# The gates of chunks 2 to 5 split between two engines in the first batch of an mLSTM and mixer kernel

## The chip, the cores and the metric

The kernel runs on one core of one Trainium2 chip. A core has five engines that work side by side, each through its own instructions in order: TensorE (PE, matmuls; PEld are its weight loads), VectorE (DVE), ScalarE (ACT), GpSimd (POOL) and SyncE (SP, which here only issues loads and stores). They meet through semaphores. SBUF is the memory on the core, PSUM the small memory that TensorE writes to. The metric is the device time of one execution in microseconds.

## The reference

Four batches, eight heads, 768 steps, head size 40. First an mLSTM layer with stabilised exponential gates, then a two-part mixer on its output.

```python
for t in range(S):                                   # the mLSTM
    m_new = max(f_gate[t] + m, i_gate[t])
    f_stab = exp(f_gate[t] + m - m_new)
    i_stab = exp(i_gate[t] - m_new)
    m = m_new
    C = f_stab * C + i_stab * outer(v[t], k[t])      # a 40x40 state for each head
    n = f_stab * n + i_stab * k[t]
    y[t] = sigmoid(o_gate[t]) * (C @ q[t]) / max(abs(n . q[t]), 1)
x  = y as (batch, 768, 320)                          # the mixer
u  = x + (relu(x.T @ w_tok1) @ w_tok2).T
out = u + relu(u @ w_ch1) @ w_ch2
```

## The kernel before

The 768 steps of a batch are cut into six chunks of 128. For a chunk the recurrence becomes matrix products: the scores of the chunk's queries and keys, weighted by a decay matrix; a product with the values; and the state carried from chunk to chunk. A pair of a batch and a chunk is a unit; u0, u1 and u2 are the first three. The mixer's matmuls fill most of the run; the first batch's six chunks come ahead of them, up to about 50 us.

The gates are computed once, for all four batches and eight heads together, with a row for each pair (36 partitions; a batch has nine, one of them spare) and the steps along the row. `gates_of` (L115) does it for a range of chunks, all on VectorE: a scan for the running maximum m (L119), the forget gate relative to it (an addition, L124, and a subtraction, L126), a scan that sums it up from each chunk's start to phi (L128, where `rst2` is zero at a chunk's first step), and two subtractions for b (L130, L132). phi and b are the two halves of the tile z. `split` (L170) then takes from the nine rows of the first batch what a bfloat16 does not hold, twice (L172, L173), so that TensorE can spread them exactly.

TensorE builds the decay matrices of the first batch from z: `spread_split` (L184) puts phi and b of one chunk into two PSUM tiles by small bfloat16 matmuls (L163, L178, L181). `prep_exp` (L282) takes their exponential on ScalarE, `st_s` (L302) makes the scores, `st_p` (L312) multiplies both on VectorE (L318), `st_pv` (L411) is the product with the values (L426), and `st_state` (L357) the state (L367, L375, L380, L384). `spread_q` (L192) spreads what decays a chunk's queries, `prep_q3` (L265) exponentiates it on ScalarE (L269) and multiplies the queries by it on GpSimd (L274, L275), and `prep_kw` (L291) weights the keys on GpSimd (L298). `x0_ops` (L459) finishes a unit on VectorE (L463 to L472). `sigmoid` (L216) does the output gates on ScalarE and needs another table of functions than the exponentials, so a table load stands ahead of it and another one behind.

No scheduler sets the order: it is written out by hand (`manual_schedule`), and each engine runs its instructions as the code lists them. So lines 831 to 857, the part between the first chunk and the loop over the others, are also the order of every engine there. In it the gates of chunk 1 are computed alone, those of chunks 2 to 5 in one go of 512 steps (L839), and `warm(7)` (L852, L788) puts seven matmuls on zeros in TensorE's way before chunk 2 is spread. At L858 `gp.release()` frees the gate tiles; weights loaded later (L616) take their place.

Of the kernel before, what the change touches and what calls it, by code (L numbers as in the profile page):

```python
# [13 lines left out]
ALU = mybir.AluOpType  # L14
# [3 lines left out]
B, H, S, D = 4, 8, 768, 40  # L18
L = 128
NC = S // L  # L20
# [14 lines left out]
def kernel(ctx: ExitStack, tc: tile.TileContext, gates, qk, q3, kv, og,  # L35
                            wt1, wt2, wc1, wc2, ident, out):
    nc = tc.nc
# [4 lines left out]
    ps_h = ctx.enter_context(tc.tile_pool(name="ps_h", bufs=2, space=PSUM))  # L42
    ps_acc = ctx.enter_context(tc.tile_pool(name="ps_acc", bufs=2, space=PSUM))
    ps_s = ctx.enter_context(tc.tile_pool(name="ps_s", bufs=2, space=PSUM))
    ps_m = ctx.enter_context(tc.tile_pool(name="ps_m", bufs=2, space=PSUM))
# [19 lines left out]
    f_t = gp.tile([B * HP, S], F32, name="f_t")  # L65
    i_t = gp.tile([B * HP, S], F32, name="i_t")
# [7 lines left out]
    z = pp.tile([128, 2, S], F32, name="z")  # L74
    nc.vector.memset(z, 0.0)
    m_t = gp.tile([B * HP, S], F32, name="m_t")
# [3 lines left out]
    rst2 = rst.rearrange("p c t -> p (c t)")  # L80
# [29 lines left out]
    phi, b_t = z[0:B * HP, 0], z[0:B * HP, 1]  # L110
# [4 lines left out]
    def gates_of(c0, c1):  # L115
        lo, hi = c0 * L, c1 * L
        sl, sd, sm = slice(lo, hi), slice(max(lo, 1), hi), slice(max(lo, 1) - 1, hi - 1)
        v = nc.vector
        v.tensor_tensor_scan(m_t[:, sl], f_t[:, sl], i_t[:, sl],  # L119
                             -1e30 if lo == 0 else m_t[:, lo - 1:lo], op0=ALU.add, op1=ALU.max)  # L120
        yield
        if lo == 0:
            v.memset(f_t[:, 0:1], 0.0)
        v.tensor_tensor(f_t[:, sd], f_t[:, sd], m_t[:, sm], ALU.add)  # L124
        yield
        v.tensor_tensor(f_t[:, sd], f_t[:, sd], m_t[:, sd], ALU.subtract)  # L126
        yield
        v.tensor_tensor_scan(phi[:, sl], rst2[:, 0:hi - lo], f_t[:, sl], 0.0, op0=ALU.mult, op1=ALU.add)  # L128
        yield
        v.tensor_tensor(b_t[:, sl], i_t[:, sl], m_t[:, sl], ALU.subtract)  # L130
        yield
        v.tensor_tensor(b_t[:, sl], b_t[:, sl], phi[:, sl], ALU.subtract)  # L132
        yield

    def cols_w0(t, c):
        a, e = c * L, (c + 1) * L
        nc.tensor.matmul(t, top(z[:, 1, a:e]), id3, start=True, stop=False)
        nc.tensor.matmul(t, top(z[:, 0, e - 1:e]).to_broadcast([128, 128]), id3, start=False, stop=True)

    def cols_w0_out(t, c):  # L140
        nc.scalar.activation(wcol[:, c, 0:HP].rearrange("p (g i) -> p i g", g=3),
                             t.rearrange("p (i g) -> p i g", i=3), AF.Exp)
# [18 lines left out]
    def spread_late(pool, tag):  # L161
        ps = pool.tile([128, 4, L], F32, tag=tag, name="ps_phi")
        nc.tensor.matmul(ps, id_b, late_b.unsqueeze(1).to_broadcast([128, 4, L]), start=True, stop=False)  # L163
        return ps


    def top(x):
        return x.bitcast(BF16).rearrange("... (t i) -> ... t i", i=2)[..., 1]

    def split(c0, c1, eng=nc.vector):  # L170
        p, r, r2 = (z[x:x + HP, :, c0 * L:c1 * L] for x in (0, 64, 96))
        eng.tensor_tensor(r, p, top(p), ALU.subtract)  # L172
        eng.tensor_tensor(r2, r, top(r), ALU.subtract)  # L173
# [10 lines left out]
    def spread_split(u, fill=0):  # L184
        T[u]["phi"] = r = []
        for h in range(0, H, 4):
            r.append(spread_late(ps_h, "h"))
            if fill and h == 0:
                warm(fill)
            spread_phi(r, u[1], h, h + 4)  # L190

    def spread_q(u, pool=(ps_h, "h")):  # L192
        b, c = u
        ps = pool[0].tile([128, 512], F32, tag=pool[1], name="ps_q")
        for g in range(3):
            nc.tensor.matmul(ps[0:120, g * L:(g + 1) * L], sel3[:, g],
                             top(z[:, 0, c * L:(c + 1) * L]), start=True, stop=True)
        T[u]["psq"] = ps[0:120, 0:3 * L].rearrange("p (g t) -> p g t", g=3)
        if c < NC - 1:
            T[u]["psw"] = ps[:, 3 * L:3 * L + HP]  # L200
            cols_w0(T[u]["psw"], c)
# [14 lines left out]
    def sigmoid(b, r=range(2), part=slice(0, 3)):  # L216
        for i in r:
            t = sig[(b, i)][:, part]
            nc.scalar.activation(t, t, AF.Sigmoid)
# [36 lines left out]
    def load_pq(u, q3t):  # L256
        b, c = u
        if c > 0:
            pq = ap.tile([120, 3, L], F32, tag="pq", name="pq", bufs=2)
            if b:  # L260
                nc.sync.dma_start(out=pq.rearrange("p g t -> p (g t)"),
                                  in_=phi_d[c, b * HP:(b + 1) * HP].rearrange("(i g) t -> i (g t)", i=3).unsqueeze(1).to_broadcast([3, D, 3 * L]))
            T[u]["q3"] = (q3t, pq)

    def prep_q3(u):  # L265
        if u[1] == 0:
            return
        q3t, pq = T[u]["q3"]
        nc.scalar.activation(pq, T[u].get("psq", pq), AF.Exp)  # L269
        if "psw" in T[u]:  # L270
            cols_w0_out(T[u]["psw"], u[1])
        if u[1] < NC - 1:
            T[u]["decay"] = a = ap.tile([120, 3], F32, tag="decay", name="decay")
            nc.gpsimd.tensor_copy(a, pq[:, :, L - 1])  # L274
        (nc.vector if u[0] == 1 else nc.gpsimd).tensor_tensor(q3t, q3t, pq, ALU.mult)  # L275
# [6 lines left out]
    def prep_exp(u, hf):  # L282
        b, c = u
        dd = T[u]["dd"]
        if b == 0:
            nc.scalar.activation(dd[:, 4 * hf:4 * hf + 4, :], T[u]["phi"][hf], AF.Exp)
            return
        for h in range(4 * hf, 4 * hf + 4):
            nc.scalar.activation(dd[:, h, :], dd[:, h, :], AF.Exp, bias=bcol[:, c, HP * b + h:HP * b + h + 1])  # L289

    def prep_kw(u):  # L291
        b, c = u
        if c == NC - 1:
            return
        t = T[u]
        kw = ap.tile([128, H * E1], F32, tag="kw", name="kw", bufs=2)
        kw = kw[:, 0:DM].rearrange("p (h d) -> p h d", d=D)
        nc.gpsimd.tensor_tensor(kw, t["kv"][:, 0:DM].rearrange("p (h d) -> p h d", d=D),  # L298
                                wcol[:, c, HP * b:HP * b + H].unsqueeze(2).to_broadcast([128, H, D]), ALU.mult)
        t["kw"] = kw  # L300

    def st_s(u, mult=True, mid=iter(()), rows=64, pool=(ps_s, "s")):  # L302
        t = T[u]
        t["s"] = [pool[0].tile([128, 4, L], F32, tag=pool[1], name="ps_sc") for _ in range(2)]
        for h in range(4):
            for hf in range(2):
                r = t["raw"][64 * hf:64 * hf + rows]
                nc.tensor.matmul(t["s"][hf][:, h, :], r[:, 1, h, :], r[:, 0, h, :], start=True, stop=True)  # L308
        if mult:
            st_p(u, mid)  # L310
# [100 lines left out]
    def st_pv(u, copy=True):  # L411
        b, c = u
        t = T[u]
        vx = t["kv"][:, DM:]
        if "p" in t:
            return st_pv3(u)
        if c:
            po = t["po"]
        else:
            t["bank"] = ps_m.tile([128, 512], F32, tag="m", name="po")  # L420
            po = t["bank"][:, 0:H * E1].rearrange("p (h e) -> p h e", e=E1)
        for h in range(H):
            o, x = po[:, h, :], vx[:, h * E1:(h + 1) * E1]
            if b == 0 and c:
                o, x = po[:, 0:h + 2:h + 1, :], x.unsqueeze(1).to_broadcast([128, 2, E1])
            nc.tensor.matmul(o, t["dd"][:, ROW[h], :], x, start=c == 0 and h == 0, stop=h == H - 1)  # L426
        if b == 0 and c:
            po = po[:, 1:1 + H]
        t["po"] = po
        if b:  # L430
            st_ht(u)
# [75 lines left out]
    u0, u1 = units[0], units[1]  # L507
# [273 lines left out]
    def step(g, n=1):  # L781
        for _ in range(n):
            next(g, None)

    def warm(n, pool=(ps_m, "m"), z=zero):
        t = pool[0].tile([128, 512], F32, tag=pool[1], name="warm")
        for i in range(n):
            nc.tensor.matmul(t[:, 0:z.shape[-1]], z[:, 0:128], z, start=i == 0, stop=i == n - 1)  # L788
# [5 lines left out]
    u0, u1, u2 = us[0:3]  # L794
# [12 lines left out]
    q3s = {u1: load_q3t(u1)}  # L807
# [23 lines left out]
    step(gates_of(1, 2), 9)  # L831
    split(1, 2)
    spread_split(u1, 5)
    st_s(u1, mult=False, pool=(ps_acc, "acc"))
    st_p(u0)
    prep_exp(u1, 0)
    prep_exp(u1, 1)
    sigmoid(0)
    step(gates_of(2, NC), 9)  # L839
    split(2, 3)  # L840
    st_pv(u0)
    x0 = x0_ops(u0)
    step(x0, 2)
    st_state(u0)
    step(x0, 1)
    spread_q(u1, (ps_s, "s"))
    load_pq(u1, q3s[u1])
    prep_q3(u1)
    prep_kw(u1)
    split(3, NC, nc.gpsimd)  # L850
    st_p(u1)
    warm(7, (ps_h, "h"))  # L852
    spread_split(u2)
    prep_exp(u2, 0)
    prep_exp(u2, 1)
# [241 lines left out]
```

## Time and profile before

| | us |
|---|---|
| median of 3 runs | 432.86 |
| lowest and highest | 432.77 and 433.51 |
| the profiled execution, whole | 433.07 |
| its span in the profile | 431.3 |
| PE busy / DVE / ACT / POOL | 425.4 / 291.9 / 185.3 / 141.7 |

The profile gives the start and the duration of every instruction in one execution; times count from the start of the span. The span covers what the engines do, and 1.8 us of the execution lie around it. A row of a timeline may stand for several instructions of one kind: `x6` is their count, and the duration is then from the first's start to the last's end. Names are the program's tiles, `out<-in`, and L is the line of the kernel. Ends of matmuls are modelled, so TensorE looks busy in places where it only waits a little; the starts are measured. The count of matmuls may be one short.

### The profile page before, as it was taken

Reading aid. Unit: us, or ns where it says so; the run is one execution under the profiler, and the core shown is the slowest. Engines: PE = TensorE matmul, PEld = TensorE weight load, DVE = VectorE, ACT = ScalarE, POOL = GpSimd, SP = SyncE. Lnnn points to the kernel's source line nnn. Section 1 sums busy time; section 2 is a strip of 40 time slices with the busy share of each in tenths; the row PEclk is TensorE's granted clock in tenths of the full one; section 3 lists DMA queues with packets and bytes.
Section 4 is the critical chain, followed back from the end, with each engine's and each line's share of the span. In section 5 each row is a group of like instructions: output and inputs, shape, how many; then the busy total and the mean of one; then the engine's idle time right before and its main releaser. Section 6 shows DMA issues by size and latency. Waiting matters only on the chain.

```text
span 431.3 us, 9405 instructions
## 1 busy us (share of the span) xinstructions
PE 425.4 (99%) x3705; PEld 408.0 (95%) x3706; DVE 291.9 (68%) x656; ACT 185.3 (43%) x426; POOL 141.7 (33%) x186
## 2 busy tenths in 40 slices
PE   8999999999999999999999999999999999999996
PEld 4788999999999999999999999999999999999996
DVE  8999877745777788688795688687885645323212
ACT  6877666894544725324414336234334112211111
POOL 7487485860553410341330330332340110000000
PEclk9999999999999999999999999999999999999999
DMA  7988849903877612145356111343240000000000
GB/s 203 278 264 250 270 142 309 291 27 112 225 218 234 204 56 81 67 130 151 96 168 195 59 64 36 125 130 100 94 115 30 2 17 15 2 32 0 27 7 30
DMA packets 24576, 52.37 MB, mean 121 GB/s; under 512 B 2565, under 2 KB 13325, under 8 KB 24533
## 3 DMA queue, kind: packets, MB, share of 16 engines
q1 hardware_dynamic: 24293, 51.61, 38.8%
q8 instruction: 29, 0.48, 0.5%
q10 hardware_dynamic: 240, 0.18, 0.2%
q14 instruction: 14, 0.11, 0.1%
HBM read 47.73 MB, written 4.04 MB: 120 GB/s over the span
## 4 chain that ended last, share of the span: by engine, by line
PE 90%; DMA 4%; DVE 2%; POOL 2%; ACT 1%; issue 1%; ACTq 0%; SPq 0%; POOLq 0%; DVEq 0%
PE ps_h L756 32%; PE acc L675 30%; PE ps_a L675 5%; PE ps_sc L308 5%; PE ps_b L675 5%; PE po L426 4%; PE po L397 3%; PE pu L375 3%; PE po L403 2%; DMA sig<-in_og_dram 2%; DMA id_t<-in_ident_dram 1%; PE po L367 1%; DMA q3t<-in_q_dram 1%; PE ps_t L737 1%; PE ps_t L735 1%
## 5 line engine op out<-in xcount | busy, mean ns | idle before, releaser
L756 PE MATMUL ps_h<-uT,c1h 128*128 128x256 f32 x720 | 137.8, 283 | 0.2
L761 ACT ACTIVATE gh<-ps_h 128x512 fp32r<-128x512 f32 x72 | 43.0, 597 | 177.8 <-PE ps_h L756 177.5
L756 PEld LDWEIGHTS ps_h<-uT,c1h 128*128 128x128 f32 x720 | 114.0, 188 | 1.4 <-DVE uT L739 0.6
L762 DVE SCALAR_TENSOR_TENSOR gl<-ps_h,gh 128x512 fp32r<-128x512 f32 x72 | 49.6, 689 | 91.6 <-ACT gh L761 91.5
L756 PE MATMUL ps_h<-uT,c1l 128*128 128x256 f32 x432 | 108.5, 281 | 0.0
L675 PE MATMUL acc<-c2h,gh 128*128 128x320 f32 x288 | 90.1, 320 | 0.0
L675 PE MATMUL acc<-c2l,gh 128*128 128x320 f32 x288 | 86.7, 309 | 0.0
L756 PEld LDWEIGHTS ps_h<-uT,c1l 128*128 128x128 f32 x432 | 79.7, 188 | 0.3 <-POOL c1l L669 0.3
L675 PE MATMUL acc<-c2h,gl 128*128 128x320 f32 x288 | 65.6, 309 | 0.0
L675 PEld LDWEIGHTS acc<-c2h,gh 128*128 128x128 f32 x288 | 54.1, 188 | 1.6
L675 PEld LDWEIGHTS acc<-c2l,gh 128*128 128x128 f32 x288 | 54.2, 188 | 0.0
L675 PEld LDWEIGHTS acc<-c2h,gl 128*128 128x128 f32 x288 | 48.1, 188 | 0.3 <-DVE gl L762 0.3
L289 ACT ACTIVATE dd<-dd,bcol 128x128 f32<-128x128 f32 x144 | 45.8, 392 | 3.7 <-POOL dd L279 3.5
L445 POOL TENSOR_TENSOR sig<-sig,ht 128x320 f32<-128x320 f32 x18 | 14.6, 814 | 94.7 <-DVE ht L407 87.7
L496 POOL TENSOR_TENSOR xl<-x,xh 128x320 fp32r<-128x320 f32 x18 | 15.8, 878 | 55.4 <-DVE xh L494 54.0
L318 DVE TENSOR_TENSOR dd<-ps_sc,dd 128x512 f32<-128x512 f32 x48 | 30.8, 680 | 1.9 <-PE ps_sc L308 1.9
L308 PE MATMUL ps_sc<-raw 64*128 64x128 f32 (+1 forms) x384 | 28.0, 285 | 0.0
L308 PEld LDWEIGHTS ps_sc<-raw 64*128 64x128 f32 (+1 forms) x384 | 23.4, 187 | 4.1 <-issue 1.9
L279 POOL TENSOR_SCALAR_AFFINE_SELECT dd<-dd 128x1024 f32<-128x1024 f32 x18 | 21.7, 1208 | 10.2 <-DMA dd<-phi_d 10.2
L426 PE MATMUL po<-kvt,dd 128*128 128x41 f32 (+1 forms) x192 | 23.2, 277 | 0.0
L426 PEld LDWEIGHTS po<-kvt,dd 128*128 128x128 f32 x192 | 22.4, 192 | 0.1
L653 DVE SCALAR_TENSOR_TENSOR pf<-pf,wst 128x384 int32<-128x384 int32 x30 | 16.2, 559 | 6.9 <-POOL wst L633 3.4
(147 smaller groups left out, 750.9 us busy)
## 6 DMA issues: line engine op xcount, KB each, us to landing
dd<-phi_d SPq DMA_DIRECT2D x18, 512.0 KB
wst<-in_wc_dram SPq DMA_DIRECT2D x22, 384.0 KB
kvt<-in_kv_dram SPq DMA_DIRECT2D x24, 324.0 KB
raw<-in_qk_dram SPq DMA_DIRECT2D x48, 160.0 KB
sig<-in_og_dram SPq DMA_DIRECT2D x8, 480.0 KB
out_dram<-x SPq DMA_DIRECT2D x24, 160.0 KB
q3t<-in_q_dram SPq DMA_DIRECT2D x20, 180.0 KB
wst<-in_wt_dram SPq DMA_DIRECT2D x8, 384.0 KB
```

Of the source, the lines that this page charges most:

```text
L279: nc.gpsimd.affine_select(dd, dd, pattern=[[0, H], [1, L]], compare_op=ALU.is_ge, fill=-1e30, base=0, channel_multiplier=-1)
L289: nc.scalar.activation(dd[:, h, :], dd[:, h, :], AF.Exp, bias=bcol[:, c, HP * b + h:HP * b + h + 1])
L308: nc.tensor.matmul(t["s"][hf][:, h, :], r[:, 1, h, :], r[:, 0, h, :], start=True, stop=True)
L318: nc.vector.tensor_tensor(dd, t["s"][hf], dd, ALU.mult)
L426: nc.tensor.matmul(o, t["dd"][:, ROW[h], :], x, start=c == 0 and h == 0, stop=h == H - 1)
L445: nc.gpsimd.tensor_tensor(sg, sg, ht[:, :, 0:D], ALU.mult)
L496: nc.gpsimd.tensor_tensor(xl, x, f32(xh), ALU.subtract)
L653: v.scalar_tensor_tensor(fi, fi, 3, raw[:, :, 0], op0=ALU.logical_shift_left, op1=ALU.bitwise_or)
L675: nc.tensor.matmul(ps, a, m, start=(first and i == 0), stop=(last and i == n - 1))
L756: nc.tensor.matmul(ps[:, j, :], c1[x][:, a:a + 128], u[:, y, :], start=part is first and i == 0 and (order == 0 or j == 0), stop=i == len( ...
L761: nc.scalar.activation(gh, ps, AF.Relu)
L762: nc.vector.scalar_tensor_tensor(gl, ps, 0.0, f32(gh), op0=ALU.max, op1=ALU.subtract)
```

## The change

A new generator, `gates_rest`, takes the place of `gates_of` for chunks 2 to 5. The running maximum is still one scan of 512 steps on VectorE. Of what follows VectorE does chunk 2 (128 steps) alone; for chunks 3 to 5 (384 steps) the two additions on f and the two subtractions on b are GpSimd's, and the scan for phi is VectorE's. Chunk 1's query factors (`spread_q`, `load_pq`, `prep_q3`) and key weights (`prep_kw`) move ahead of the sigmoids, the spread of the queries right behind that of phi and into another PSUM pool. The second split of chunks 3 to 5 moves up a little, and the seven matmuls on zeros go.

```diff
--- before.py
+++ after.py
@@ -130,6 +130,24 @@
         v.tensor_tensor(b_t[:, sl], i_t[:, sl], m_t[:, sl], ALU.subtract)
         yield
         v.tensor_tensor(b_t[:, sl], b_t[:, sl], phi[:, sl], ALU.subtract)
+        yield
+
+    def gates_rest():
+        v, p = nc.vector, nc.gpsimd
+        a, z = slice(2 * L, 3 * L), slice(3 * L, S)
+        am, zm = slice(2 * L - 1, 3 * L - 1), slice(3 * L - 1, S - 1)
+        v.tensor_tensor_scan(m_t[:, 2 * L:], f_t[:, 2 * L:], i_t[:, 2 * L:], m_t[:, 2 * L - 1:2 * L],
+                             op0=ALU.add, op1=ALU.max)
+        for e, s, sm in ((v, a, am), (p, z, zm)):
+            e.tensor_tensor(f_t[:, s], f_t[:, s], m_t[:, sm], ALU.add)
+            e.tensor_tensor(f_t[:, s], f_t[:, s], m_t[:, s], ALU.subtract)
+        v.tensor_tensor_scan(phi[:, a], rst2[:, 0:L], f_t[:, a], 0.0, op0=ALU.mult, op1=ALU.add)
+        v.tensor_tensor(b_t[:, a], i_t[:, a], m_t[:, a], ALU.subtract)
+        v.tensor_tensor(b_t[:, a], b_t[:, a], phi[:, a], ALU.subtract)
+        yield
+        p.tensor_tensor(b_t[:, z], i_t[:, z], m_t[:, z], ALU.subtract)
+        v.tensor_tensor_scan(phi[:, z], rst2[:, 0:S - 3 * L], f_t[:, z], 0.0, op0=ALU.mult, op1=ALU.add)
+        p.tensor_tensor(b_t[:, z], b_t[:, z], phi[:, z], ALU.subtract)
         yield
 
     def cols_w0(t, c):
@@ -831,25 +849,26 @@
     step(gates_of(1, 2), 9)
     split(1, 2)
     spread_split(u1, 5)
+    spread_q(u1, (ps_m, "m"))
     st_s(u1, mult=False, pool=(ps_acc, "acc"))
     st_p(u0)
     prep_exp(u1, 0)
     prep_exp(u1, 1)
+    gr = gates_rest()
+    step(gr)
+    load_pq(u1, q3s[u1])
+    prep_q3(u1)
+    prep_kw(u1)
     sigmoid(0)
-    step(gates_of(2, NC), 9)
     split(2, 3)
+    step(gr)
+    split(3, NC, nc.gpsimd)
     st_pv(u0)
     x0 = x0_ops(u0)
     step(x0, 2)
     st_state(u0)
     step(x0, 1)
-    spread_q(u1, (ps_s, "s"))
-    load_pq(u1, q3s[u1])
-    prep_q3(u1)
-    prep_kw(u1)
-    split(3, NC, nc.gpsimd)
     st_p(u1)
-    warm(7, (ps_h, "h"))
     spread_split(u2)
     prep_exp(u2, 0)
     prep_exp(u2, 1)
```

The first place is VectorE, from the maximum's scan (which stands here as a SCALAR_TENSOR_TENSOR) up to x0 of the first unit (L463 before, L481 after). Before:

```order
L119 SCALAR_TENSOR_TENSOR m_t<-f_t,m_t,i_t 36x512
L124 TENSOR_TENSOR f_t<-f_t,m_t 36x512
L126 TENSOR_TENSOR f_t<-f_t,m_t 36x512
L128 SCALAR_TENSOR_TENSOR z<-rst,f_t 36x512
L130 TENSOR_TENSOR z<-i_t,m_t 36x512
L132 TENSOR_TENSOR z<-z 36x512
L172 TENSOR_TENSOR z<-z 9x2x128
L173 TENSOR_TENSOR z<-z 9x2x128
L463 TENSOR_TENSOR po<-po,sig 128x8x40
```

After, with the lines of the changed file:

```order
L139 SCALAR_TENSOR_TENSOR m_t<-f_t,m_t,i_t 36x512
L142 TENSOR_TENSOR f_t<-f_t,m_t 36x128
L143 TENSOR_TENSOR f_t<-f_t,m_t 36x128
L144 SCALAR_TENSOR_TENSOR z<-rst,f_t 36x128
L145 TENSOR_TENSOR z<-i_t,m_t 36x128
L146 TENSOR_TENSOR z<-z 36x128
L190 TENSOR_TENSOR z<-z 9x2x128
L191 TENSOR_TENSOR z<-z 9x2x128
L149 SCALAR_TENSOR_TENSOR z<-rst,f_t 36x384
L481 TENSOR_TENSOR po<-po,sig 128x8x40
```

Five instructions on 512 steps have become five on chunk 2's 128, ahead of the same split of chunk 2; a scan on 384 steps has come in behind the split.

The second place is GpSimd, from the filling of a tile with zeros (the memset) to chunk 0's xl. Before:

```order
L214 MEMSET raw_138 32x1024 x2
L274 COPY decay<-pq 120x3
L275 TENSOR_TENSOR q3t<-q3t,pq 120x384
L298 TENSOR_TENSOR kw<-kvt,wcol 128x320
L172 TENSOR_TENSOR z<-z 9x2x384
L173 TENSOR_TENSOR z<-z 9x2x384
```

After:

```order
L232 MEMSET raw_138 32x1024 x2
L142 TENSOR_TENSOR f_t<-f_t,m_t 36x384
L143 TENSOR_TENSOR f_t<-f_t,m_t 36x384
L292 COPY decay<-pq 120x3
L293 TENSOR_TENSOR q3t<-q3t,pq 120x384
L316 TENSOR_TENSOR kw<-kvt,wcol 128x320
L148 TENSOR_TENSOR z<-i_t,m_t 36x384
L150 TENSOR_TENSOR z<-z 36x384
L190 TENSOR_TENSOR z<-z 9x2x384
L191 TENSOR_TENSOR z<-z 9x2x384
```

Two instructions on f_t stand ahead of chunk 1's query factors and key weights, and two on z between these and the split of chunks 3 to 5; both kinds wait for VectorE at their head.

## Rows read from the trace of the kernel before

**Rows 1.** Timeline of PE: start us, duration us, engine, line, operation, count, [idle before]

```profile
15.33 1.67 PE L788 MATMUL warm<-zero 128*128 128x512 bf16 x6
...
17.18 0.39 PE L178 MATMUL ps_phi<-z,id 128*128 128x128 bf16 x4
```

**Rows 2.** Timeline of DVE, same columns, 10.9 to 17.7 us

```profile
10.97 1.27 DVE L119 TENSOR_TENSOR_SCAN m_t<-f_t,m_t,i_t 36x512 f32<-36x512 f32 x1
...
13.71 1.22 DVE L128 TENSOR_TENSOR_SCAN z<-rst,f_t 36x512 f32<-36x512 f32 x1
...
16.71 0.42 DVE L173 TENSOR_TENSOR z<-z 9x256 f32<-9x256 f32 x1
17.16 0.50 DVE L463 TENSOR_TENSOR po<-po,sig 128x320 f32<-128x320 f32 x1
```

**Rows 3.** Waits of DVE, 17 to 34 us: total us, times, longest us

```profile
DVE pf L653 <- ACT wst L631: 0.6, 1, 0.6
```

**Rows 4.** Timeline of DVE, 25 to 34 us

```profile
32.69 0.49 DVE L472 TENSOR_TENSOR x<-po,den 128x320 f32<-128x320 f32 x1
```

**Rows 5.** Timeline of PE, 31 to 34 us

```profile
33.28 0.80 PE L375 MATMUL pu<-kvt,kw 128*120 128x123 f32 x6 [0.71 <-POOL w1l L669]
```

**Rows 6.** Windows: stretch, length, busy us (instructions) by engine, clock, DMA

```profile
42.00:150.00 108.00, 107.87 (x881) 104.75 (x880) 75.20 (x168) 68.44 (x163) 59.72 (x75) 1.00 0.67 206
428.00:432.00 4.00, 0.02 (x1) 0.00 (x0) 0.49 (x1) 0.00 (x0) 0.00 (x0) 0.81 0.22 82
```

**Rows 7.** Timeline of DVE, 5.4 to 9.8 us

```profile
5.94 0.68 DVE L119 TENSOR_TENSOR_SCAN m_t<-f_t,m_t,i_t 36x128 f32<-36x128 f32 x1
6.65 0.48 DVE L124 TENSOR_TENSOR f_t<-f_t,m_t 36x128 f32<-36x128 f32 x1
7.17 0.28 DVE L126 TENSOR_TENSOR f_t<-f_t,m_t 36x128 f32<-36x128 f32 x1
7.49 0.42 DVE L128 TENSOR_TENSOR_SCAN z<-rst,f_t 36x128 f32<-36x128 f32 x1
...
8.89 0.84 DVE L173 TENSOR_TENSOR z<-z 9x256 f32<-9x256 f32 x1
```

**Rows 8.** Timeline of POOL, 5.5 to 9.6 us

```profile
5.59 0.77 POOL L106 TENSOR_SCALAR_AFFINE_SELECT bm_t<-bm_t 120x369 f32<-120x369 f32 x1
...
6.43 0.58 POOL L106 TENSOR_SCALAR_AFFINE_SELECT bm_t<-bm_t 120x369 f32<-120x369 f32 x1
...
8.73 0.72 POOL L298 TENSOR_TENSOR kw<-kvt,wcol 128x320 f32<-128x320 f32 x1 [1.68 <-ACT wcol L141]
```

**Rows 9.** Timeline of DVE, 149 to 152.7 us

```profile
150.56 0.74 DVE L349 CAST v<-vr 128x328 bf16<-128x328 f32 x1
151.33 1.27 DVE L350 TENSOR_TENSOR v<-vr,v 128x328 bf16<-128x328 f32 x1
```

**Rows 10.** Timeline of POOL, 149 to 152.7 us

```profile
150.12 0.98 POOL L298 TENSOR_TENSOR kw<-kvt,wcol 128x320 f32<-128x320 f32 x1
151.06 1.18 POOL L279 TENSOR_SCALAR_AFFINE_SELECT dd<-dd 128x1024 f32<-128x1024 f32 x1
```

**Rows 11.** Tile vr on DVE: duration ns min/median/max, first and last start us

```profile
L350 DVE TENSOR_TENSOR v<-vr,v x12: 499/501/1267, 151.3 to 334.5; 128x328 bf16<-128x328 f32 x12
```

**Rows 12.** Lines of POOL: instructions xcount | busy us, mean ns | idle before

```profile
L275 POOL TENSOR_TENSOR q3t<-q3t,pq 120x384 f32<-120x384 f32 x15 | 15.2, 1016 | 0.0
...
L147 POOL TENSOR_TENSOR w_row<-z 36x640 f32<-36x640 f32 x1 | 1.3, 1257 | 0.0
```

**Rows 13.** Timeline of ACT, 10.8 to 21 us

```profile
14.66 1.00 ACT L219 ACTIVATE sig<-sig 128x960 f32<-128x960 f32 x1 [0.18 <-DMA sig<-in_og_dram]
...
16.97 0.49 ACT L269 ACTIVATE pq<-ps_q 120x384 f32<-120x384 f32 x1
...
17.82 1.26 ACT L286 ACTIVATE dd<-ps_phi 128x512 f32<-128x512 f32 x2 [0.28 <-PE ps_phi L181]
```

**Rows 14.** Timeline of PE, 1 to 6 us

```profile
1.39 4.45 PE L788 MATMUL warm<-zero 128*128 128x512 bf16 x10 [1.39 <-POOL zero L60]
```

## The prediction

> **What bounds the kernel now.** I read the timelines of the first 35 us first, since the change lies between 5 and 23 us, then the waits of VectorE, then the windows of the rest, to see whether a delay made early comes out at the end.
>
> TensorE stands on zeros from 15.33 until about 17.0 and spreads phi of u2 at 17.18 [rows 1]. VectorE's second split of chunk 2 ends at 16.71 + 0.42 = 17.13 [rows 2], and that is what the zeros cover: a wait for VectorE. Right behind it, at 17.16, VectorE starts L463, the first instruction on u0's output. From there to 33.18, the end of L472 on u2 [rows 4], its only wait of note is 0.6 us, once, on ScalarE [rows 3], and ScalarE gets that work from VectorE's own earlier one. So VectorE bounds 17 to 33 us. The view of TensorE at 33.28 puts a wait of 0.71 us down to GpSimd's w1l [rows 5], but the matmul pu does not read w1l; L472 ended 0.1 us before it and frees the PSUM that pu takes. I read this as TensorE waiting for VectorE. After 42 us TensorE is busy for 107.87 of 108 us [rows 6]: what it is late there it does not make up. A shift of L463 on VectorE therefore moves the end one for one, unless TensorE itself becomes the later one.
>
> **The change part by part.** *VectorE alone.* The scan for m stays and ends at 10.97 + 1.27 = 12.24 [rows 2]; with the gap of 0.03 that lies between two VectorE instructions the next starts at 12.27. Before, 4.9 us of 512-step work and splits followed up to 17.16. After, there are an addition and a subtraction on f, a scan, two subtractions on b, all on 128 steps, and the two splits: by the undisturbed rows of chunk 1 0.28 for an addition or subtraction, 0.42 for a scan [rows 7], and 0.42 for a split [rows 2]. That is 4 × 0.28 + 3 × 0.42 + 7 gaps of 0.03 = 2.6. Then the scan on 384 steps: between 0.42 for 128 [rows 7] and 1.22 for 512 [rows 2] it is 0.95. L463 would start at 15.8, 1.35 us sooner.
>
> *What GpSimd does beside it.* It now has, in this order and from 12.24 on, f+ and f− (384 steps), decay, q3t, kw and b − m, all reading SBUF, while every VectorE instruction of the gates and splits has two inputs in SBUF. Rows 7 and 8 show what such neighbours do. The scan of chunk 1 took 0.68 and ended at 6.62, 0.26 after the affine_select on GpSimd (6.36); the addition took 0.48 and ended 0.12 after the next one (7.01); the split took 0.84 and ended 0.28 after kw (9.45). Alone they take 0.42, 0.28 and 0.42. So VectorE stood still until GpSimd's instruction was over, and only its first 0.14 or so passed beside it. It holds the other way too: at 150 us GpSimd's L279 ended 0.94 after VectorE's L349 did (151.30), and VectorE's L350 ended 0.36 after L279 (152.24), at 1.27 where it mostly takes 0.50 [rows 9 to 11]; kw's L298 there took 0.98 [rows 10] where it took 0.72 [rows 8]. Two queues that both have work take turns, one instruction each.
>
> The Trainium skill, SBUF — State Buffer, "Who interferes with whom", says that a VectorE instruction with two SBUF inputs contends with a GpSimd instruction that reads SBUF, and that whoever comes second waits for the whole of the other. This case's trace agrees on who contends, but shows about 0.14 us of each passing beside the other; without that the sum would be 1.4 us higher.
>
> *The price of a GpSimd instruction on 384 steps* is not in the trace. The nearest rows are q3t, the same 384 elements in a row, in place and from two fp32 inputs, 1.02 on average, and w_row on the same 36 partitions, 640 elements, 1.26 [rows 12]. In proportion the latter gives 0.76 for 384; in full it is a bound from above. I take 1.0, from q3t, which has the same operation and length. Less 0.14 each holds VectorE 0.86 (0.62 and 1.12 at the bounds); kw holds it 0.72 − 0.14 = 0.58.
>
> The Trainium skill, GPSIMD Engine Reference, "3.1 Elementwise — side-by-side cycle accounting", gives 4497 ns for an addition of 2048 fp32 elements. My estimate from that page is 0.84 for 384, and the sum would be 0.5 us lower by it; no run here shows it.
>
> *The sum, in turns from 12.27*, VectorE's remainders being the time alone less 0.14: addition 0.28 (it is there first), f+ 0.86, subtraction 0.14, f− 0.86, scan 0.28, b − m 0.26 (beside it only decay, 120x3, for which I add 0.05), q3t 0.86, b − phi 0.14, kw 0.58, first split 0.28, GpSimd's b − m 0.86, second split 0.28. This is GpSimd 4.02 + decay 0.05 + VectorE 1.66 = 5.73. The split of chunk 2 ends at 18.0, not 17.13, so TensorE's spread of u2 comes 0.85 later instead of earlier. Behind the split VectorE has the scan of 384 steps, 0.95, and two gaps; nothing holds it, because GpSimd's b − phi waits for that scan. L463 starts at 19.0 against 17.16: **1.85 later**. Three of the holds have the unknown price; at 0.62 each the sum is 0.72 lower (+1.1), at 1.12 it is 0.78 higher (+2.6). The profiled execution would go from 433.07 to 434.9; it lay 0.21 above the median, so the forecast against 432.86 is 434.7.
>
> *Edits that I cost at nothing.* ScalarE has the same instructions ahead of u2's exponential in another order, two small ones ahead of the sigmoids; the whole row of them was done at 17.54, when it waited 0.28 for TensorE [rows 13], and the spread that it waits for is now later still. Without that cover the cost would be at most their 0.7. The three matmuls of `spread_q` move forward on TensorE, in time that it then waits through. The seven matmuls on zeros (1.67, [rows 1]) go from a stretch in which TensorE waits anyway. The wait that is added on GpSimd, f+ for the m scan, has decay, q3t and kw of u1 queued behind it; they are wanted by u1's products, which follow st_p(u1) on VectorE and so shift with it. b − phi waits for the 384-step scan, and behind it is the split of chunks 3 to 5, at 19.9 to about 22.9; TensorE wants it for the spread of u3, which is itself late by about as much. SP's weight loads wait longer for the freed gate tiles, 1.4 to 1.7 us; their readers shift by about the same.
>
> **Rivals.**
>
> *A, the engines do not hold each other here* (the other side: faster). Against it stand rows 7 to 11, for it only that none of those pairs is a 36x384 one. L463 needs the sigmoid. This ended at 15.66 and gets the exponential of pq, 0.49 [rows 13], and a smaller one put ahead of it, so L463 cannot start before about 16.2: −1.0. And u2's exponential cannot start before 17.54, which is only 0.28 sooner [rows 13]. So −0.3 to −1.0, in the middle 432.2. It decides if the split of chunk 2 ends before about 16.
>
> *B, VectorE passes more than one instruction in a turn.* If GpSimd waits by itself between its instructions (q3t's query load, kw for ScalarE, the start of f− behind f+), VectorE slips two in. Two turns fewer take 2 × 0.86 away: +0.1 to +0.3, 433.1. For it: the undisturbed pair at 7.17 and 7.49, when GpSimd was idle [rows 7]; against it, that GpSimd has almost all inputs from the start.
>
> *C, the clock.* TensorE idles from about 15.3 to 18.0, and no matmuls on zeros fill this. Idle at the end of the run, it shows a granted clock of 0.81 [rows 6], and at the start ten such matmuls took 4.45 us, some 0.44 each [rows 14], against seven in 1.67, some 0.24 [rows 1]: the lower level, 1.2 against 2.4 GHz. If it starts at 18.0 on the lower level for as long a stretch as that 4.45, it loses half of this, 2.2, on top of the 0.85: +3.0, 435.9. It decides when TensorE is later than VectorE by 33 us. Against it: the wait is only about 1 us longer than the 1.67 that the zeros filled.
>
> **How the numbers follow.** The forecast (alternation, +1.1 to +2.6, so 434.0 to 435.5) gets 0.63, since three separate pairs and one sequence of four show it; A 0.12, B 0.15, C 0.10. The time is 434.7. The range must take in B, and it reaches up to C's value, for the upper price of GpSimd and a little of the clock: 432.8 to 435.9; A below it and half of C above it, with the forecast's own tails, are about 0.19. A change of less than 0.2%, 0.87 us, can't be told from none here. Faster by more is half of A and a little for what I don't see: 0.09. Within it are the other half of A, B, and 0.02 of the forecast's lower tail: 0.23. Slower: 0.68.
>
> **What would show it.** In the profile of the changed kernel the 384-step instructions of GpSimd take 1.0 or more each (L142, L143, L148), and VectorE's instructions beside them end 0.12 to 0.3 after GpSimd's. The second split of chunk 2 (L191) ends at about 18.0, the scan at L149 takes 0.95 undisturbed, x0 of u0 (L481) starts near 19.0, and TensorE's pu of u3 comes near 35. The prediction is wrong if L143 to L191 take 0.28 and 0.42 while GpSimd works (A), if two of them lie between neighbouring GpSimd instructions (B), if the granted clock after 15 us is below 1 (C), or if VectorE shows a wait between 19 and 35 us that swallows the delay.

## The result and the profile after

The changed kernel took 436.46 us (median of 4 executions, 435.97 to 437.72), the kernel before 433.04: 0.8% slower, ratio 1.0079, interval 1.0067 to 1.0091. That is 3.4 us where 1.85 were forecast, and 0.56 above the range. The profiled execution took 437.72 us, with a span of 436.0 against 431.3, so its own loss is the largest of the four.

VectorE first, in the timeline of the changed kernel: start, duration, engine, line, operation.

```profile
11.12 1.27 DVE L139 TENSOR_TENSOR_SCAN m_t<-f_t,m_t,i_t 36x512 f32<-36x512 f32 x1
12.42 0.28 DVE L142 TENSOR_TENSOR f_t<-f_t,m_t 36x128 f32<-36x128 f32 x1
12.74 0.97 DVE L143 TENSOR_TENSOR f_t<-f_t,m_t 36x128 f32<-36x128 f32 x1
13.74 1.36 DVE L144 TENSOR_TENSOR_SCAN z<-rst,f_t 36x128 f32<-36x128 f32 x1
15.03 1.02 DVE L145 TENSOR_TENSOR z<-i_t,m_t 36x128 f32<-36x128 f32 x1
16.09 0.69 DVE L146 TENSOR_TENSOR z<-z 36x128 f32<-36x128 f32 x1
16.82 1.10 DVE L190 TENSOR_TENSOR z<-z 9x256 f32<-9x256 f32 x1
17.95 0.42 DVE L191 TENSOR_TENSOR z<-z 9x256 f32<-9x256 f32 x1
18.40 0.95 DVE L149 TENSOR_TENSOR_SCAN z<-rst,f_t 36x384 f32<-36x384 f32 x1
19.27 0.47 DVE L481 TENSOR_TENSOR po<-po,sig 128x320 f32<-128x320 f32 x1
```

And GpSimd beside it:

```profile
12.53 1.04 POOL L142 TENSOR_TENSOR f_t<-f_t,m_t 36x384 f32<-36x384 f32 x1 [1.68 <-issue]
13.64 0.99 POOL L143 TENSOR_TENSOR f_t<-f_t,m_t 36x384 f32<-36x384 f32 x1
...
14.73 1.17 POOL L293 TENSOR_TENSOR q3t<-q3t,pq 120x384 f32<-120x384 f32 x1
15.87 0.76 POOL L316 TENSOR_TENSOR kw<-kvt,wcol 128x320 f32<-128x320 f32 x1
16.60 1.03 POOL L148 TENSOR_TENSOR z<-i_t,m_t 36x384 f32<-36x384 f32 x1
```

f+ and f− are GpSimd's L142 and L143, the addition and the subtraction on f; its b − m is L148. Read the two engines by the ends of their instructions. f+ ends at 13.57 and VectorE's L143 at 13.71; q3t at 15.90 and L145 at 16.05; kw at 16.63 and L146 at 16.78; b − m at 17.63 and L190 at 17.92. Each of these four VectorE instructions takes 0.3 to 0.4 alone [rows 2, 7]. One pair differs: f− ends at 14.63 and the scan L144 at 15.10, 0.47 later, so the whole of the 0.42 that this scan takes alone came behind f−. The last split, L191, finds GpSimd waiting for VectorE and takes 0.42. So the split of chunk 2 ends at 18.37 instead of 17.13, and x0 of u0 starts at 19.27, 2.1 us later than in the kernel before [rows 2].

Now TensorE, in the same kernel:

```profile
15.53 0.38 PE L181 MATMUL ps_phi<-late_b,id_b 128*128 128x512 bf16 x1
18.42 0.58 PE L196 MATMUL ps_phi<-z,id 128*128 128x128 bf16 x4 [2.51 <-DVE z L191]
...
37.31 0.80 PE L393 MATMUL pu<-kvt,kw 128*120 128x123 f32 x6 [0.68 <-POOL w1l L687]
```

The four matmuls that spread phi take 0.58 where they took 0.39 [rows 1]: the clock. The windows show it (length, busy us of PE, PEld, DVE, ACT, POOL, then the granted clock):

```profile
15.00:16.00 1.00, 0.91 (x8) 0.63 (x8) 1.00 (x2) 0.98 (x2) 1.00 (x2) 1.00 0.76 188
17.00:18.00 1.00, 0.00 (x0) 0.00 (x0) 0.97 (x2) 0.19 (x1) 0.63 (x1) 0.89 0.99 346
18.00:24.00 6.00, 5.58 (x35) 4.28 (x35) 5.46 (x13) 2.28 (x6) 4.27 (x4) 0.50 0.75 250
24.00:25.00 1.00, 1.00 (x9) 1.00 (x8) 0.10 (x1) 1.00 (x3) 1.00 (x3) 0.70 0.20 72
```

TensorE did nothing from 15.9 to 18.4; its granted clock fell to half, 1.2 GHz, at about 17.8 and was whole again after some 24.6. And in this time VectorE, which waited for nothing but 0.6 us before [rows 3], has two new waits for TensorE, the first and the third of these (total us, times, longest):

```profile
DVE pu L398 <- PE pu L393: 1.3, 1, 1.3
DVE pf L671 <- POOL w1l L687: 0.6, 1, 0.6
DVE dd L336 <- PE ps_sc L326: 0.4, 1, 0.4
```

They are 1.7 us together, on top of the 2.1. x0 of u1 starts 3.97 later than before; first the kernel before, then the changed one:

```profile
23.91 0.48 DVE L463 TENSOR_TENSOR po<-po,sig 128x320 f32<-128x320 f32 x1
```
```profile
27.88 0.48 DVE L481 TENSOR_TENSOR po<-po,sig 128x320 f32<-128x320 f32 x1
```

pu of u3 comes at 37.31, not 33.28 [rows 5]. After 42 us TensorE has almost as few gaps as before (107.57 of 108 us busy, 107.87 before), so nothing is made up.

### The profile page after: what moved, and what is told of

The parts are those of the page before. It is cut to its first block, busy times and chain, and to the rows that moved or that the text cites. A ratio compares the mean times of both kernels' runs of the same rounds, so it can differ in the third digit from the quotient of the medians.

```text
span 436.0 us, 9396 instructions
## 1 busy us (share of the span) xinstructions
PE 426.8 (98%) x3699; PEld 409.6 (94%) x3699; DVE 293.7 (67%) x657; ACT 184.8 (42%) x426; POOL 145.3 (33%) x190
## 4 chain that ended last, share of the span: by engine, by line
PE 87%; DVE 5%; DMA 2%; POOL 2%; ACT 2%; issue 1%; DVEq 0%; POOLq 0%; ACTq 0%
PE ps_h L774 29%; PE acc L693 27%; PE ps_sc L326 5%; PE ps_a L693 5%; PE ps_b L693 5%; PE po L444 4%; PE po L415 3%; PE pu L393 3%; DMA wst<-in_wc_dram 2%; PE po L421 2%; PE po L385 2%; POOL c1l L687 1%; PE ps_t L755 1%; PE ps_t L754 1%; PE ps_t L753 1%
## 5 line engine op out<-in xcount | busy, mean ns | idle before, releaser
L463 POOL TENSOR_TENSOR sig<-sig,ht 128x320 f32<-128x320 f32 x18 | 14.7, 815 | 96.3 <-DVE ht L425 88.5
L326 PE MATMUL ps_sc<-raw 64*128 64x128 f32 (+1 forms) x384 | 29.7, 292 | 0.2 <-DMA raw<-in_qk_dram 0.2
L326 PEld LDWEIGHTS ps_sc<-raw 64*128 64x128 f32 (+1 forms) x384 | 24.7, 193 | 4.6 <-issue 1.9
```

What stands on the lines that cost most here:

```text
L463: nc.gpsimd.tensor_tensor(sg, sg, ht[:, :, 0:D], ALU.mult)
```

## The experiments

Each was timed against the kernel before on the same chip. "x0 of u0" is its start on VectorE in the profiled execution (17.16 in the kernel before), "clock" the mean granted clock of the timed executions (0.998 to 1.0 in the 70 executions of the kernel before, but for one with 0.996 and 435.56 us). Rows with the same time before ran on one chip. The ratio is worked out from all executions and is not quite that of the two medians.

| kernel | median us | before | ratio, interval | x0 of u0 | clock |
|---|---|---|---|---|---|
| changed, again | 435.99 | 433.39 | 1.0065, 1.0053 to 1.0077 | 19.10 | 0.991 to 0.996 |
| changed, 12 zeros | 435.73 | 433.68 | 1.0044, 1.0032 to 1.0056 | 19.34 | 0.999 to 1.0 |
| changed, 7 zeros | 435.06 | 433.68 | 1.0033, 1.0021 to 1.0045 | 19.15 | 1.0 |
| before, no zeros | 433.73 | 433.68 | 0.9999, 0.9990 to 1.0008 | 17.16 | 0.991 to 1.0 |
| changed, all gates on VectorE | 435.33 | 433.68 | 1.0044, 1.0028 to 1.0060 | 18.93 | 0.988 to 1.0 |
| before, GpSimd reads | 435.02 | 433.77 | 1.0034, 1.0019 to 1.0050 | 18.97 | 0.999 to 1.0 |
| before, GpSimd writes | 433.73 | 433.77 | 1.0004, 0.9993 to 1.0016 | 17.17 | 0.999 to 1.0 |
| before, q factors first | 435.14 | 433.39 | 1.0047, 1.0035 to 1.0059 | 19.55 | 0.998 to 1.0 |
| changed, q factors late | 433.55 | 433.39 | 1.0011, 1.0002 to 1.0019 | 17.96 | 0.999 to 1.0 |
| own, b − m early | 434.22 | 433.77 | 1.0032, 1.0009 to 1.0055 | 15.00 | 0.988 to 1.0 |
| own, b − m late | 434.94 | 433.77 | 1.0040, 1.0016 to 1.0064 | 14.88 | 0.991 to 1.0 |
| own, third | 433.09 | 433.39 | 0.9997, 0.9987 to 1.0007 | 14.89 | 0.999 to 1.0 |

**The clock: zeros put back.**

```diff
     st_p(u1)
+    warm(7, (ps_h, "h"))        # and, in another kernel, warm(12, ...)
     spread_split(u2)
```

> The changed kernel with twelve matmuls on zeros ahead of the spread of u2 (it has none there). Theory, two causes that add: VectorE and GpSimd take turns, which starts x0 of u0 2.1 us later (19.27 against 17.16), and TensorE runs at half clock from about 18 to 24.5 us, because it stood idle from 15.9 to 18.4, which makes VectorE wait for it once more. With zeros in the idle time the granted clock stays at 1.0, x0 of u0 stays near 19.3, x0 of u1 comes near 26.0 (27.9 in the changed kernel, 23.9 before), and the time is about 435.1. Rival, the turns on VectorE and what they delay are all of it: the clock costs nothing that is not covered, 436.4 as the changed kernel.

> The changed kernel with the seven matmuls on zeros that stood there before. They end near 17.2, and 1.2 us of idle time follow. If what TensorE did before its clock falls is a longer idle stretch than that, the result is that of the run with twelve, 435.1. If any idle stretch of about 1 us there is enough, the clock falls later and the time lies between 435.1 and 436.4. The rival (clock costs nothing) expects 436.4.

With seven zeros VectorE is as late as in the changed kernel, and the clock stays whole, also behind the 1.08 us for which TensorE still waits:

```profile
18.00:24.00 6.00, 5.70 (x60) 5.08 (x60) 5.83 (x15) 4.07 (x9) 4.39 (x4) 1.00 0.80 265
```
```profile
18.30 0.39 PE L196 MATMUL ps_phi<-z,id 128*128 128x128 bf16 x4 [1.08 <-DVE z L191]
```

TensorE starts 60 matmuls between 18 and 24 us, where the changed kernel started 35. x0 of u1 starts here at

```profile
25.87 0.48 DVE L481 TENSOR_TENSOR po<-po,sig 128x320 f32<-128x320 f32 x1
```

1.96 later than in the kernel before (23.91), so the delay of u0 is handed on unchanged and no new one is added. Twelve zeros do the same (26.05); the intervals of the two times overlap. The rival (it costs nothing) falls: both versions end below the changed kernel, measured against the kernel before on the chip of each.

**The changed kernel again.** It ran on another chip than the versions with zeros, so these are compared through the kernel before, which was timed on both.

> The changed kernel once more, on the chip on which the next three run. Theory: TensorE is idle for about 2.5 us ahead of u2's spread, its clock falls in every execution (mean granted clock of the execution 0.992 to 0.997, where the kernel before shows 0.999 to 1.0), 3.0 to 3.6 us slower than before; the two versions with matmuls on zeros were 1.4 and 2.0 slower. Rival (the difference to those two was the chip): as they, 1.4 to 2.0 slower.

The five executions had clocks of 0.991 to 0.996, as the first four (0.992 to 0.996); in the runs with zeros none was below 0.999. So the clock falls in all nine executions of the changed kernel. How long it stays low differs. In this profile TensorE was idle for 3.0 us, and the clock was low from about 18.2 to 21.6:

```profile
18.00:19.00 1.00, 0.76 (x5) 0.53 (x5) 0.97 (x2) 0.00 (x0) 0.00 (x0) 0.58 0.67 254
...
21.00:22.00 1.00, 1.00 (x16) 0.95 (x12) 1.00 (x3) 0.54 (x2) 0.92 (x2) 0.71 0.93 312
```

VectorE's wait for u1's pu is then 0.4 us, and x0 of u1 starts at 26.39, 2.48 late, 0.54 more than x0 of u0. In the first profile, with 6.8 us of low clock (17.8 to 24.6), it was 3.97 late, 1.86 more than x0 of u0. The time, 2.6 to 2.8 above before, lies somewhat below what I expected (3.0 to 3.6) and above both versions with zeros, though the interval of its ratio just meets that of the twelve. So the two profiles put the clock's price at 0.5 and 1.9 us. The other executions have no profile, and why the clock comes back sooner in one than in the other is open.

**The zeros alone.** The kernel before without `warm(7, (ps_h, "h"))`.

> The kernel before without its seven matmuls on zeros, nothing else. TensorE is idle from about 15.4 to 17.1, 1.7 us. Theory: in the changed kernel the clock fell after some 2 us of idle time, so here it may just hold; then 433.0 as before. If it falls here too, TensorE runs at half clock from 17 to about 23 us and the time is 435 or so, although VectorE is as early as before. The prediction's own step (the zeros go from a stretch in which TensorE waits anyway, at no cost) expects 433.0.

By the twelve executions there is no difference. But two of them had a lower clock: 0.991 with 435.90 us, and 0.996 with 434.03. The profile is of the first, and shows x0 of u0 unmoved at 17.16 while TensorE runs at half clock:

```profile
16.00:17.00 1.00, 0.00 (x0) 0.00 (x0) 0.93 (x3) 0.97 (x3) 0.00 (x0) 0.73 0.97 341
17.00:22.00 5.00, 4.82 (x33) 3.52 (x32) 3.62 (x11) 1.55 (x3) 4.75 (x5) 0.50 0.86 264
```

x0 of u1 then starts at

```profile
26.61 0.48 DVE L463 TENSOR_TENSOR po<-po,sig 128x320 f32<-128x320 f32 x1
```

2.70 late, though x0 of u0 is in time: the price of the clock in this execution, more than in either profile of the changed kernel. TensorE waited 2.0 us for VectorE in this execution; the others have no profile. So the zeros could go for nothing in ten executions of twelve. It is the longer wait together with their removal that costs in every execution.

**GpSimd's reads, and its writes.** Into the kernel before, behind GpSimd's memset at 11.5 us:

```diff
     zero_rows(0)
+    scr = gp.tile([36, 512], F32, name="scr")
+    for _ in range(2):                             # in the other kernel: range(4)
+        nc.gpsimd.tensor_tensor(scr[:, 0:384], rst2[:, 0:384], rst2[:, 0:384], ALU.mult)
+                                                   # in the other: nc.gpsimd.memset(scr, 0.0)
```

The first one also has twelve zeros instead of seven.

> The kernel before with two additional products of 36x384 elements on GpSimd, from SBUF into a scratch tile, behind its memset at 11.5 us, beside VectorE's gates, and twelve instead of seven matmuls on zeros, so that TensorE's clock has no part in it. Theory (turns): each holds VectorE for 0.86 us, x0 of u0 starts at about 18.9 instead of 17.16, and the time is 1.7 us above the kernel before. Rival (the instructions of the changed kernel were slow for another reason, as the shape of 128 steps or waits of GpSimd's own): VectorE as in the kernel before, 17.16, no change of the time.

> The kernel before with four additional memsets of 36x512 elements on GpSimd at the same place, some 2 us that only write SBUF. Theory (turns are taken where both read SBUF): VectorE is not held, x0 of u0 stays at 17.16, no change. Rival (any work of GpSimd holds VectorE): four holds of some 0.4 us, x0 of u0 at about 18.7, 1.5 us more.

With the reads, VectorE:

```profile
12.29 1.13 DVE L124 TENSOR_TENSOR f_t<-f_t,m_t 36x512 f32<-36x512 f32 x1
13.45 1.20 DVE L126 TENSOR_TENSOR f_t<-f_t,m_t 36x512 f32<-36x512 f32 x1
...
17.69 1.25 DVE L173 TENSOR_TENSOR z<-z 9x256 f32<-9x256 f32 x1
18.97 0.50 DVE L463 TENSOR_TENSOR po<-po,sig 128x320 f32<-128x320 f32 x1
```

With the writes, VectorE and GpSimd:

```profile
12.28 0.68 DVE L124 TENSOR_TENSOR f_t<-f_t,m_t 36x512 f32<-36x512 f32 x1
...
17.17 0.50 DVE L463 TENSOR_TENSOR po<-po,sig 128x320 f32<-128x320 f32 x1
```
```profile
10.75 2.25 POOL L824 MEMSET scr<- 36x512 f32 x4
```

The writes ran until 13.0, beside the maximum's scan and L124, and held nothing. The reads lengthened L124 and L126 by 0.45 and 0.52, not by 0.86 each, and pushed the last split (L173) into the turn of u1's q factors, 0.83 more: 1.8 together. The mechanism is as expected. That the sum is too is luck in part: the two reads alone cost 0.97 of the 1.72 expected, and the third hold I had not counted. The Trainium skill, SBUF — State Buffer, "Who interferes with whom", exempts GpSimd instructions that only write; the trace agrees (0.68 with and without them).

**The two halves of the change.** First the q factors alone, in the kernel before, with twelve zeros:

```diff
     spread_split(u1, 5)
+    spread_q(u1, (ps_m, "m"))
...
+    load_pq(u1, q3s[u1])
+    prep_q3(u1)
+    prep_kw(u1)
     sigmoid(0)
...
     step(x0, 1)
-    spread_q(u1, (ps_s, "s"))
-    load_pq(u1, q3s[u1])
-    prep_q3(u1)
-    prep_kw(u1)
     split(3, NC, nc.gpsimd)
```

> The kernel before with one part of the change: chunk 1's query factors and key weights ahead of the sigmoids; gates as before on VectorE, twelve matmuls on zeros, so that the clock has no part. Theory (turns): q3t and kw on GpSimd now run at 13.2 to 15.5 beside VectorE's 512-step gates and hold them for 0.86 and 0.58: x0 of u0 at about 18.6 instead of 17.16, 1.0 to 1.5 us slower. Rival (the move is neutral, as its own code suggests: GpSimd idled there): no change.

x0 of u0 starts at 19.55, later than expected, and even later than in the changed kernel. VectorE and GpSimd:

```profile
13.76 1.92 DVE L128 TENSOR_TENSOR_SCAN z<-rst,f_t 36x512 f32<-36x512 f32 x1
15.61 1.14 DVE L130 TENSOR_TENSOR z<-i_t,m_t 36x512 f32<-36x512 f32 x1
...
17.95 1.57 DVE L173 TENSOR_TENSOR z<-z 9x256 f32<-9x256 f32 x1
```
```profile
13.26 1.34 POOL L275 TENSOR_TENSOR q3t<-q3t,pq 120x384 f32<-120x384 f32 x1 [0.82 <-DMA q3t<-in_q_dram]
14.55 1.65 POOL L298 TENSOR_TENSOR kw<-kvt,wcol 128x320 f32<-128x320 f32 x1
17.61 1.63 POOL L172 TENSOR_TENSOR z<-z 9x768 f32<-9x768 f32 x1 [1.41 <-DVE z L132]
```

q3t and kw hold it for 0.70 and 0.48, somewhat less than the 0.86 and 0.58 of the theory, and L173 takes 1.57 because GpSimd, done with the q factors, starts the split of chunks 3 to 5 (1.63) in between: 1.15 that I had not counted. Then the gates alone:

```diff
-    load_pq(u1, q3s[u1])       # ahead of sigmoid(0); and spread_q ahead of st_s(u1)
-    prep_q3(u1)
-    prep_kw(u1)
...
     step(gr)
-    split(3, NC, nc.gpsimd)
...
     step(x0, 1)
+    spread_q(u1, (ps_s, "s"))
+    load_pq(u1, q3s[u1])
+    prep_q3(u1)
+    prep_kw(u1)
+    split(3, NC, nc.gpsimd)
     st_p(u1)
+    warm(7, (ps_h, "h"))
```

> The changed kernel with chunk 1's query factors and key weights where they were before, and with the seven matmuls on zeros. Theory (turns): of the holds f+, f- and b - m are left, 3 x 0.86 against the 2.3 us by which VectorE's own work is shorter ahead of the split; the split of chunk 2 ends near 16.9, x0 of u0 starts near 17.9, 0.7 us later than before; the time is 0.3 to 0.8 us above before. Rival (GpSimd's gates carry the whole loss of 2 us): x0 of u0 near 19.2.

Here x0 of u0 starts at 17.96, as the ledger of turns had it (17.9), with three holds left, and the kernel is 0.1% slower than before, at the edge of what can be told. So the move of the q factors, which looked like the harmless part, is the dearer of the two by itself. The two do not add (2.4 and 0.8 alone, 2.1 together), since each changes what GpSimd has ready at VectorE's turns.

**All gates on VectorE.** The four instructions of GpSimd's gates go to VectorE, behind the second split of chunk 2; no zeros.

```diff
-        for e, s, sm in ((v, a, am), (p, z, zm)):
-            e.tensor_tensor(f_t[:, s], f_t[:, s], m_t[:, sm], ALU.add)
-            e.tensor_tensor(f_t[:, s], f_t[:, s], m_t[:, s], ALU.subtract)
+        v.tensor_tensor(f_t[:, a], f_t[:, a], m_t[:, am], ALU.add)
+        v.tensor_tensor(f_t[:, a], f_t[:, a], m_t[:, a], ALU.subtract)
...
-        p.tensor_tensor(b_t[:, z], i_t[:, z], m_t[:, z], ALU.subtract)
+        v.tensor_tensor(f_t[:, z], f_t[:, z], m_t[:, zm], ALU.add)       # and so on, all on v
```

> The changed kernel with the gates of chunks 3 to 5 on VectorE, behind the second split of chunk 2; GpSimd has only chunk 1's q factors and key weights beside chunk 2's gates, and no matmuls on zeros are added. Theory: the split of chunk 2 ends near 16.2 instead of 18.4 (two holds, 0.86 and 0.58, are left), TensorE is idle for less than 1 us and its clock stays at 1.0; VectorE has five instructions on 384 steps ahead of x0 of u0, which starts near 19.3 as in the changed kernel. So VectorE is as late and the clock is whole: 435.1. If the clock does not matter: 436.4, since VectorE is as late. If GpSimd's gates alone made the loss: about 433.

The split of chunk 2 ends at 15.92, TensorE waits 0.43 for it, but x0 of u0 starts at 18.93, and the time is 1.65 above before. The forecast of this run holds for the time. What it does not separate cleanly is the clock: TensorE then waits 2.0 us at the next place, for u1's state (the view names GpSimd's split, which that matmul does not read; VectorE's Cn ends at 20.5, just ahead of it), and two of the eight executions show a mean clock of 0.988 and 0.992, where I expected it to stay whole. In the profiled one it did (0.999):

```profile
PE po L386 <- POOL z L191: 2.0, 1, 2.0
...
PE ps_phi L197 <- DVE z L192: 0.4, 1, 0.4
```

**An order of my own.** If the turns are what costs, GpSimd's gates belong beside those instructions of VectorE that have one input in PSUM. So the maximum, the gates and the split of chunk 2 are done alone, and f+ and f− of chunks 3 to 5 run beside u0's output. There are three versions. This is the edit of the second; the first has b − m right behind f− on GpSimd (`step(gr, 2)`), the third has the scan of phi ahead of u1's q factors and the split of chunks 4 and 5 behind u2's key weights.

```diff
-    step(gates_of(2, NC), 9)
+    step(gates_of(2, 3), 9)
     split(2, 3)
+    gr = gates_rest()          # v: scan of m on 384 steps; p: f+, f-; later p: b - m, v: scan, p: b - phi
+    step(gr)
...
-    split(3, NC, nc.gpsimd)
     st_p(u1)
-    warm(7, (ps_h, "h"))
+    step(gr, 9)
+    split(3, 4, nc.gpsimd)
+    split(4, NC, nc.gpsimd)
     spread_split(u2)
```

> The kernel before with the gates of chunk 2 alone, their maximum too (a scan of 128 steps), then the split of chunk 2; only then the scan of the maximum for chunks 3 to 5, and GpSimd's f+, f- and b - m beside VectorE's work on u0's output, which has one input in PSUM; phi's scan of 384 steps behind st_p of u1, the split of chunk 3 ahead of that of chunks 4 and 5; no matmuls on zeros. Theory (turns only where VectorE has two inputs in SBUF): the split of chunk 2 ends near 14.1 without a hold, TensorE has no idle time there, x0 of u0 starts near 15.1 instead of 17.16, but u1's q factors come 0.7 us later than before on GpSimd; 0.5 to 1.2 us faster than before if these don't take it back, 432.5. Rival (GpSimd's q factors and splits become the bound, since it has three gate instructions ahead of them): the spread of u3 waits for GpSimd's split, same or up to 1 us slower.

> As the run above, but b - m behind u1's q factors and key weights on GpSimd, so that these are as early as before. Theory: TensorE's state product of u1 is not later, the split of chunk 3 ends near 21.5 to 22.5, in time for u3's spread at about 22; 0.8 to 1.2 us faster than before. Rival as above: the split is late, the spread of u3 waits, same.

> As own_b_late, but phi's scan ahead of u1's q factors on GpSimd, the split of chunk 3 ahead of xl of u0, and the rest (b - phi and the split of chunks 4 and 5) behind u2's key weights. Theory: VectorE is not held in its scan, GpSimd's q factors of u2 are no later than in the kernel before, u3's spread waits at most 0.6 us; 0 to 0.7 us faster than before. Rival (GpSimd stays the bound, 4 us of gates have come to it): u3's spread or u4's waits for its split, 0 to 1 us slower.

x0 of u0 does start at 14.9 to 15.0, 2.2 us sooner than in the kernel before, and no instruction of chunk 2's gates is held. x0 itself (L479 here), with one input in PSUM, is not held by f+ either; in the third:

```profile
14.89 0.47 DVE L479 TENSOR_TENSOR po<-po,sig 128x320 f32<-128x320 f32 x1
```
```profile
15.10 1.00 POOL L141 TENSOR_TENSOR f_t<-f_t,m_t 36x384 f32<-36x384 f32 x1 [4.10 <-issue]
```

But u1's x0 starts at 24.04 in the first and 24.50 in the third, against 23.91; in the second it starts at 23.31, and TensorE then waits 1.2 us for GpSimd's split and 1.6 for its q factors. In the first TensorE waits 1.6 us for GpSimd's q factors. So in these two GpSimd has become the bound, as the rival said. In the third VectorE's scan of phi meets u1's q factors and key weights and waits for both, against what I expected, and TensorE then waits 0.9 us for pu of u2:

```profile
17.19 2.55 DVE L144 TENSOR_TENSOR_SCAN z<-rst,f_t 36x384 f32<-36x384 f32 x1 [0.36 <-POOL f_t L142]
...
26.44 0.48 DVE L488 TENSOR_TENSOR x<-po,den 128x320 f32<-128x320 f32 x1
```
```profile
PE pu L391 <- POOL z L188: 0.9, 1, 0.9
```

The view names GpSimd's split of chunks 4 and 5, but pu does not read z. pu starts at 27.02, 0.1 behind the end of VectorE's L488, as it does behind L472 in the kernel before; I read this as a wait for VectorE, which the long scan had made late.

The first two are slower than before, and some of their executions show the low clock too. In the first these are four of twelve (0.988 to 0.995, 435.25 to 438.30 us), and the other eight took 433.46 to 434.53; no profile shows where the clock fell. The third is the same as before (0.9997): I did not find a version that beats it.

## Why the prediction was wrong

The direction was right, and so was the path: VectorE's turns with GpSimd, then one for one to the end. By the steps:

- *GpSimd's price on 384 steps*, taken as 1.0 from q3t: 1.04, 0.99 and 1.03. The estimate from the Trainium skill, GPSIMD Engine Reference, "3.1 Elementwise — side-by-side cycle accounting", was 0.84; here the measurement decides.
- *The ledger of turns*: split of chunk 2 at 18.0, measured 18.37, of which 0.15 is a later end of the maximum's scan (12.39, not 12.24) and 0.19 the scan L144, which ended 0.47 behind f− where the ledger gave it 0.28. The order of the turns was another (L145, not L146, met q3t, and L191 was free), but the same five instructions of GpSimd came ahead of the split's end. The scan on 384 steps: 0.95, measured 0.95 too. x0 of u0 at 19.0: 19.27, and 19.10 when it ran again. The two dummy reads, the memsets and the gates alone bear the mechanism out; the price of a single hold varied, from 0.41 to 0.94 in the changed kernel.
- *One for one to the end*: with the clock whole, x0 of u1 is 1.96 late (seven zeros) and 2.14 (twelve), and the time 1.4 and 2.05 above before, against 1.85 forecast. From the start of u3's pu to the end of the span it takes 398.0 us in the kernel before and 397.6 to 399.1 in the other profiles, whether pu is late or not. This part alone would have ended inside the range.
- *The step that failed* is the edit costed at nothing: "The seven matmuls on zeros (1.67, [rows 1]) go from a stretch in which TensorE waits anyway." They were not idle filling. The ledger itself had made that stretch longer, to the 2.5 to 3.0 us that TensorE now stood idle, and behind it the clock falls, with a mean of 0.991 to 0.996 in all nine executions seen. It is the forecast's own delay that takes away the cover of another edit. I had this as rival C, but beside the forecast instead of on top of it, with a chance of 0.10, and argued that the wait is "only about 1 us longer than the 1.67 that the zeros filled". That comparison left out that none of the wait was filled any more. In the two profiles this put 1.9 and 0.5 us on top of VectorE's delay, and with zeros put back nothing.
- *Rival C's price*, +3.0 in all, was close to the 3.4 of the first result and the 2.6 of the second, but by other terms: about 2.0 from VectorE and, in the two profiles, 1.9 and 0.5 from the clock, where I had 0.85 and 2.2. That the sums are alike is luck.
- *Rival A* (faster) is excluded: L143 to L190, ahead of the last split, took 0.69 to 1.36, not 0.28 and 0.42. *B*, two turns fewer, did not occur. In one kernel the opposite did (below).

## What to carry to other kernels

Work that moves to GpSimd is not free for VectorE where VectorE's instructions beside it read two operands from SBUF: here a GpSimd instruction of 0.7 to 1.0 us mostly cost VectorE 0.4 to 0.9. Put it beside instructions that read PSUM, and count what was already on GpSimd and is now pushed into such a place too. Matmuls on zeros that cover a wait are not idle filling: without them the clock fell in two of twelve executions even where nothing else was changed, and in all nine of the changed kernel, where the wait was longer. When an estimate makes such a wait longer, the clock belongs in that estimate as a term, not as a rival.

## What was not expected

- VectorE can lose two turns in one instruction. In the changed kernel with twelve zeros its scan of chunk 2 took 2.26 us, over f− and q3t, which stood on GpSimd with only the small decay copy between them:

```profile
13.60 2.26 DVE L144 TENSOR_TENSOR_SCAN z<-rst,f_t 36x128 f32<-36x128 f32 x1
```
```profile
13.49 1.00 POOL L143 TENSOR_TENSOR f_t<-f_t,m_t 36x384 f32<-36x384 f32 x1
14.44 0.18 POOL L292 COPY decay<-pq 120x3 f32<-120x3 f32 x1
14.59 0.99 POOL L293 TENSOR_TENSOR q3t<-q3t,pq 120x384 f32<-120x384 f32 x1
```

  With seven zeros, and with none, the same scan got through between the two, at 1.36. In my third order the scan of phi lost two turns as well (2.55 where it takes 0.95). So the turns are not strict; what decides is open.
- In these runs the length of an idle stretch alone does not settle what the clock does. In the kernel before without zeros it fell in two of twelve executions, one of which the profile shows, with 2.0 us of idle time; with all gates on VectorE the profile shows 2.0 us as well, and the clock stayed whole. In the changed kernel it fell in nine of nine, in two of which the profile shows 2.5 and 3.0 us, and it stayed low for 6.8 us in the first of these and for 3.4 in the other.
